# First slots of a fused attention, SoLU layer and gated layer kernel: softmax beside the first layer of the tile in front, values ahead of the next scores, products with x's low part last, w_out copies moved up

## The chip, the cores and the metric

The kernel runs on one core of one Trainium2 chip. The metric is the device time of one execution in microseconds (us). Engines are called as in the profile: PE is TensorE's matmul, PEld its weight load, DVE is VectorE, ACT is ScalarE, POOL is GpSimd, SP is SyncE, from whose queue most DMAs are issued.

## What is computed

Three layers follow one another on 4608 tokens: attention within chunks of 64 tokens (8 batches, 8 heads, head width 64), a layer with a softmax-weighted hidden vector and a layer norm, and a gated layer. Inputs q, k, v and g_ln are float32 as used here; the weights w_in, w_out, w_gate, w_val and w_out2 arrive as 8-byte numbers.

```python
scores = scale * np.matmul(q_c, k_c.transpose(0, 1, 2, 4, 3))
attn = np.exp(scores - max) ; attn = attn / (sum + 1e-09)
x = np.matmul(attn, v_c)            # 4608 x 512
h = x @ w_in                        # 4608 x 1024
sm = softmax(h); solu = h * sm
ln = (solu - mu) / np.sqrt(var + 1e-06) * g_ln
y = ln @ w_out                      # 4608 x 512
out = (silu(y @ w_gate) * (y @ w_val)) @ w_out2   # d_ff 1536
```

## The kernel before, in words

Tokens are taken as 36 tiles of 128; three tiles are a group. The first phase works through the tiles in slots, one for each t from 0 to 35; the second phase (from about 590 us on) is the gated layer over what the first phase left in DRAM.

Each float product is made of three: every operand is split into a high part and a low part (what the high part leaves over), and `PASSES` (L148) names the three products high by high, high by low, low by high.

The work on one tile t is a chain over four engines:

- `scores(t)` (L276): 32 small matmuls on PE into `s_ps`. `s_ps` and `o_ps` are two halves of one PSUM tile `so_ps` (L254, L255), and there is only one of it.
- `softmax(t)` (L281): DVE maximum (L283), DVE subtraction (L285), ACT exponential (L289). `softmax_b(t)` (L292): DVE sum, epsilon, reciprocal (L295, L296, L298), and the multiplication on POOL (L299).
- `p_transpose(t)` (L303): four PE transposes (L307) and an ACT copy p (L309). `pv(t)` (L312): 32 small matmuls with v into `o_ps`.
- `x_split(t)` (L317): ACT copies the high part of x (L321) and a DVE subtraction makes the low part, called later (L323).
- `hidden(t)` (L330): two halves of 12 products of 512 columns (L339) into the one PSUM tile `h`; in each half, for every k, high by high, high by low, low by high, in this order.
- `ln_max(t)` (L351, DVE), `ln_exp(t)` (L358, ACT), `ln_b(t)` (L364 to L373, DVE; its product at L369 is the last to read `h`), `ln_c(t)` (L379 on ACT, then seven instructions on POOL, L381 to L393).
- `ln_T(t)` (L409 on PE, L412 on ACT, and low parts on DVE, L417, called later).
- `y_run` (L155): products of the finished groups with w_out, `wB`, from slot 4 on (`Y_AT`).

Beside this the weights are converted from their 8-byte form: `conv_start` (L81, L87 on ACT, L94 on POOL) for the units of the next slot, `conv_b` (L100, L108 on DVE), `conv_c` (L129 on POOL), and for w_out `split_scaled` (L143 on ACT, L144 on DVE), which puts them into `wB`. Of w_out there are 8 units: one in each of the slots 0 to 3 and two in each of 4 and 5. A slot hands its units to the next as `todo2`; `steps[1]` is what calls `split_scaled` there. Units 0 to 3 hold the left half of w_out's columns (the first two y of a group), 4 to 7 the right half.

The order of instructions on each engine is written out by hand: from L506 on, every engine runs its instructions in the order in which the functions are called, and only data and buffers make it wait. In slots 0 to 3 (`first_slot`, L651) the order on PE is scores(t+2), pv(t+1), hidden(t), p_transpose(t+2), ln_T(t-1). In slots 4 to 35 (`slot`, L602) it is scores(t+2), hidden(t), ln_T(t-1), pv(t+1), y, p_transpose(t+2).

Loads go by SP's queue in the order of the calls: q and k of tile t+4, v of tile t+3, and at the end of a slot the raw weights for slot t+2.

Of the kernel before, what the change touches and what calls it, by code (L numbers as in the profile page):

```python
# [21 lines left out]
Y_AT = 4  # L22
# [4 lines left out]
def attn_moe_moe2_kernel(  # L27
# [13 lines left out]
    nc = tc.nc  # L41
# [4 lines left out]
    DM = 512  # L46
    KD = DM // P
# [100 lines left out]
    PASSES = ((0, 0), (0, 1), (1, 0))  # L148
# [37 lines left out]
    def w2_out(u):  # L186

        f, j = divmod(u, 3)
        if j == 0:
            gates[f] = stage.tile([P, 2, KH], F32, tag="ga", name="ga", bufs=2)  # L190
            return gates[f]
        if j == 1:
            blks[f] = stage.tile([P, 6, KH], F32, tag="blk", name="blk", bufs=1)
            return blks[f][:, 0:6:5]
# [43 lines left out]
    with ExitStack() as ph1:  # L238
        wpool = ph1.enter_context(tc.tile_pool(name="wpool", bufs=1))
        wA = wblock(wpool, "A", 2 * KD)  # L240
# [25 lines left out]
        def load_qk(t):  # L266
            qt[t] = att.tile([P, H, CH], F32, tag="qt", name="qt")
            nc.sync.dma_start(out=qt[t], in_=qT[t].rearrange("p (h i) -> p h i", h=H))
            kt[t] = att.tile([P, H, CH], F32, tag="kt", name="kt")
            nc.sync.dma_start(out=kt[t], in_=kT[t].rearrange("p (h j) -> p h j", h=H))  # L270

        def load_v(t):
            vt[t] = att.tile([P, H, CH], F32, tag="vt", name="vt")
            nc.sync.dma_start(out=vt[t], in_=v[t].rearrange("p (h d) -> p h d", h=H))

        def scores(t):  # L276
            q, k = qt.pop(t), kt.pop(t)
            for i in quads:
                quad(s_ps, q, k, *i)

        def softmax(t):  # L281
            mx = sm.tile([P, 2, NP], F32, tag="mx", name="mx")
            nc.vector.tensor_reduce(out=mx, in_=s_ps, axis=AX.X, op=ALU.max)  # L283
            e = att.tile([P, H, CH], F32, tag="e", name="e")
            nc.vector.tensor_tensor(  # L285
                out=e.rearrange("p (n c) j -> p c n j", c=2), in0=s_ps,
                in1=mx.unsqueeze(3).to_broadcast([P, 2, NP, CH]), op=ALU.subtract,
            )
            nc.scalar.activation(out=e, in_=e, func=AF.Exp, scale=SCALE)  # L289
            st[t] = e  # L290
# [21 lines left out]
        def pv(t):  # L312
            vv, p = vt.pop(t), st.pop(("p", t))
            for i in quads:
                quad(o_ps, vv, p, *i)

        def x_split(t):  # L317
            o = o_ps.rearrange("p c n i -> p n c i")
            x = xp.tile([P, 2, KD, P], F32R, tag="x", name="x")
            hi, lo = (x[:, i].rearrange("p n (c i) -> p n c i", c=2) for i in range(2))  # L320
            nc.scalar.activation(out=hi, in_=o, func=AF.Copy)  # L321
            xt[t] = x
            low = lambda: nc.vector.tensor_tensor(  # L323
                out=lo, in0=o, in1=hi.bitcast(F32), op=ALU.subtract
            )
            return low
# [3 lines left out]
        def hidden(t, halves=(0, 1)):  # L330
            x = xt[t]
            if 0 in halves:
                ht[t] = ps_h.tile([P, DF], F32, tag="h", name="h")
            h = ht[t]
            for n in halves:
                i = 0
                for k in range(KD):
                    for a, b in PASSES:
                        nc.tensor.matmul(  # L339
                            h[:, n * DM:(n + 1) * DM], lhsT=x[:, a, k, :],  # L340
                            rhs=wA[:, n * KD + k, b, :],
                            start=(i == 0), stop=(i == 3 * KD - 1),
                        )
                        i += 1
            if 1 in halves:
                del xt[t]

# [202 lines left out]
        x_low = x_split(0)  # L550
# [28 lines left out]
        x_low = x_split(1)  # L579
# [22 lines left out]
        def slot(t, todo2):  # L602


            todo, ahead = w_todo(t), t + 2 < NT
            cs = conv.pop(t)
            outs = [w2_out(u) if k == "2" else None for k, u in todo]
            if ahead:
                scores(t + 2)
                if t + 4 < NT:  # L610
                    load_qk(t + 4)
                softmax(t + 2)
            cs[:1] = [conv_c(c, o) for c, o in zip(conv_b(cs[:1]), outs)]
            if ahead:
                softmax_b(t + 2)
            if t > 0:
                hidden(t)
            ln_max(t)
            ln_exp(t)
            for k, steps in todo2:  # L620
                steps[0]()
            ln_low = ln_T(t - 1) if t >= 1 else None
            ln_b(t)
            x_low = None
            if t + 1 < NT:
                pv(t + 1)
                if t + 3 < NT:
                    load_v(t + 3)
                x_low = x_split(t + 1)
            if ln_low:  # L630
                ln_low()
            if x_low:
                x_low()
            ln_c(t)
            y0, y1 = y_upto(t - 1), y_upto(t)
            y2 = min(y1, -(-y0 // NY) * NY)
            y_run(wB, y0, y2, ps_y, att)
            for k, steps in todo2:
                steps[1]()
            if t + 1 < NT:  # L640
                conv_start(t + 1)
            cs[1:] = [conv_c(c, o) for c, o in zip(conv_b(cs[1:]), outs[1:])]
            y_run(wB, y2, y1, ps_y, att)
            for k, steps in todo2:
                steps[2]()
            if t + 2 < NT:
                raws[t + 2] = w_raw(t + 2)
                p_transpose(t + 2)
            return w_rest(todo, cs)

        def first_slot(t, todo2):  # L651


            todo = w_todo(t)
            cs = conv.pop(t)

            def attend():
                scores(t + 2)
                load_qk(t + 4)
                for k, steps in todo2:  # L660
                    steps[1]()
                softmax(t + 2)

            load_v(t + 3)
            if t > 0:
                attend()
                pv(t + 1)
                x_split(t + 1)()
                softmax_b(t + 2)
                conv_start(t + 1)  # L670
                hidden(t)
                p_transpose(t + 2)
            ln_max(t)
            ln_exp(t)
            cs = [conv_c(c) for c in conv_b(cs)]
            ln_low = ln_T(t - 1) if t > 0 else None
            ln_b(t)
            if t == 0:
                attend()
            if ln_low:  # L680
                ln_low()
            ln_c(t)
            if t == 0:
                softmax_b(t + 2)
                p_transpose(t + 2)
                conv_start(t + 1)
            raws[t + 2] = w_raw(t + 2)
            return w_rest(todo, cs)
# [254 lines left out]
```

## Time and profile before

| what | value |
|---|---|
| median of 3 runs | 1433.0 us (1431.76 to 1435.57) |
| the profiled execution, its own time | 1431.88 us |
| its span in the trace | 1430.1 us |
| PE busy | 1349.3 us, 94% of the span |
| DVE, ACT, POOL busy | 844.2, 565.5, 469.7 us |
| mean granted clock of TensorE | 0.982 |

The page cuts the span into 40 slices of 35.75 us. PE is busy for 90% or more of nearly every slice from the fifth on; the second and third slices, in which the first slots lie, are the ones with idle PE. A time "from the start" below is from the start of the span. In rows of the timeline, the bracket gives how long the engine was idle before the instruction and what ended that.

### The profile page before, as it was taken

To read this page: it belongs to the slowest core of one execution; us is meant where nothing else is said; L and a number is where in the kernel's file an instruction comes from. 1 tells how busy PE (TensorE), PEld (TensorE's weight loads), DVE (VectorE), ACT (ScalarE), POOL (GpSimd) and SP (SyncE) were. 2 spreads that over 40 slices of the span, in tenths; PEclk is the share of its full clock that TensorE was granted. 3 is DMA by queue.
4 is the path that set the end of the run, shared out by engine and by line. 5 is a ranking of instruction groups with operands and counts; after the bars stand their busy time and mean duration, and the time that the engine had idled before them with its cause. 6 is when DMAs were issued, how large, how long until landed. Compare 5 with 4: busy or idle time off the path is not lost.

```text
span 1430.1 us, 23605 instructions
## 1 busy us (share of the span) xinstructions
PE 1349.3 (94%) x9072; PEld 1231.2 (86%) x9072; DVE 844.2 (59%) x1540; ACT 565.5 (40%) x1144; POOL 469.7 (33%) x590
## 2 busy tenths in 40 slices
PE   3378999999999999899999999999999999999998
PEld 2367988888888889899989998999999999989997
DVE  6558577667777776455465456445544654474442
ACT  5346456446464545432242233223323323233231
POOL 5335354444545444421231223213212412141120
PEclk9689999999999999999999999999999999999999
DMA  6233265645555543886645473455455454735531
GB/s 235 67 118 108 77 207 164 205 153 196 175 194 177 190 146 119 302 319 231 232 145 190 173 241 138 173 195 210 148 198 205 156 189 166 246 127 181 202 106 45
DMA packets 91328, 252.15 MB, mean 176 GB/s; under 512 B 8272, under 2 KB 42064, under 8 KB 82000
## 3 DMA queue, kind: packets, MB, share of 16 engines
q1 hardware_dynamic: 84304, 241.21, 48.9%
q10 hardware_dynamic: 6912, 9.44, 1.9%
q8 instruction: 72, 1.18, 0.3%
q14 instruction: 40, 0.33, 0.1%
HBM read 203.43 MB, written 47.19 MB: 175 GB/s over the span
## 4 chain that ended last, share of the span: by engine, by line
PE 70%; DVE 2%; DMA 2%; ACT 1%; POOL 1%; issue 1%; ACTq 0%; SPq 0%; DVEq 0%; POOLq 0%
PE o L841 14%; PE pa L775 11%; PE pd L775 10%; PE pc L775 10%; PE tail L841 7%; PE h L339 6%; PE pb L775 5%; PE y L163 5%; PE so_ps L261 1%; PE tr L409 1%; DMA wsa<-ws 1%; DMA y<-ysb 1%; PE pt L307 1%; DVE so L369 0%; DVE nm L351 0%
## 5 line engine op out<-in xcount | busy, mean ns | idle before, releaser
L339 PE MATMUL h<-wA,x 128*128 128x512 f32 x864 | 217.0, 408 | 8.5 <-DVE x L323 2.8
L163 PE MATMUL y<-lnT,wB 128*128 128x384 f32 x1152 | 213.9, 343 | 9.4 <-ACT wB L143 5.7
L163 PEld LDWEIGHTS y<-lnT,wB 128*128 128x128 f32 x1152 | 202.6, 191 | 12.6 <-ACT wB L143 6.3
L832 POOL TENSOR_TENSOR uflow<-sa,uflow 128x384 fp32r<-128x384 f32 x72 | 73.4, 1019 | 414.0 <-ACT uflow L803 392.9
L339 PEld LDWEIGHTS h<-wA,x 128*128 128x128 f32 x864 | 165.7, 196 | 47.0 <-DVE x L323 3.6
L775 PE MATMUL pa<-yk,wsa 128*128 128x384 f32 x864 | 175.2, 337 | 3.4 <-ACT p L800 2.6
L775 PE MATMUL pd<-yk,wsb 128*128 128x384 f32 x864 | 173.0, 334 | 0.0
L832 DVE TENSOR_TENSOR uflow<-sb,uflow 128x128 fp32r<-128x128 f32 x72 | 28.1, 390 | 228.8 <-ACT uflow L830 228.8
L775 PEld LDWEIGHTS pa<-yk,wsa 128*128 128x128 f32 x864 | 153.2, 188 | 10.5 <-ACT p L800 2.9
L775 PEld LDWEIGHTS pd<-yk,wsb 128*128 128x128 f32 x864 | 151.8, 188 | 0.0
L811 POOL TENSOR_TENSOR u<-u,p 128x384 f32<-128x384 f32 x72 | 72.9, 1013 | 196.3 <-DVE u L810 183.7
L800 ACT ACTIVATE p<-pa 128x384 f32<-128x384 f32 x72 | 35.4, 492 | 234.1 <-PE pa L775 230.8
L841 PE MATMUL o<-wo,uflow 128*128 128x512 f32 x504 | 122.8, 392 | 0.0
L841 PEld LDWEIGHTS o<-wo,uflow 128*128 128x128 f32 x504 | 94.1, 188 | 18.0
L358 ACT ACTIVATE eh<-h,nm 128x1024 f32<-128x1024 f32 x36 | 40.2, 1117 | 143.7 <-DVE nm L351 143.7
L813 ACT ACTIVATE sa<-pa 128x384 f32<-128x384 f32 x72 | 35.4, 492 | 149.1 <-PE pa L775 149.1
L841 PE MATMUL o<-uflow 128*128 128x512 f32 x360 | 87.5, 392 | 0.0
L775 PE MATMUL pc<-yk,wsa 128*128 128x384 f32 x432 | 86.5, 334 | 0.0
L775 PE MATMUL pb<-yk,wsa 128*128 128x384 f32 x432 | 86.5, 334 | 0.0
L775 PE MATMUL pc<-yk,wsb 128*128 128x384 f32 x432 | 86.5, 334 | 0.0
L814 DVE TENSOR_TENSOR sa<-pa,sa 128x384 f32<-128x384 f32 x72 | 40.2, 558 | 71.5 <-ACT sa L813 71.5
L841 PEld LDWEIGHTS o<-uflow 128*128 128x128 f32 x360 | 67.3, 188 | 13.1
(106 smaller groups left out, 2282.6 us busy)
## 6 DMA issues: line engine op xcount, KB each, us to landing
wsa<-ws SPq DMA_DIRECT2D x72, 1024.0 KB, 5.1
wsb<-ws SPq DMA_DIRECT2D x72, 768.0 KB, 6.0
ws<-shi SPq DMA_DIRECT2D x12, 896.0 KB, 4.4
raw<-in_moe_w_out SPq DMA_DIRECT2D x20, 512.0 KB, 6.6
qt<-in_q SPq DMA_DIRECT2D x36, 256.0 KB, 4.1
kt<-in_k SPq DMA_DIRECT2D x36, 256.0 KB, 4.0
vt<-in_v SPq DMA_DIRECT2D x36, 256.0 KB, 2.8
y<-ysb ACTq DMA_DIRECT2D x48, 192.0 KB, 2.4
```

The costliest lines, as they stand in the source:

```text
L163: nc.tensor.matmul(ys[u], lhsT=wB[:, f, a, d * P:(d + 1) * P], rhs=lnT[m][:, b, f, :], start=(n == 0), stop=(n == NY - 1),)
L261: nc.tensor.matmul(out[b * CH:(b + 1) * CH, c, n], lhsT=lhsT[r, h], rhs=rhs[r, h], start=True, stop=True, tile_position=(c * CH, b * CH),)
L307: nc.tensor.transpose(pt[:, 2 * n:2 * n + 2].rearrange("p h i -> p (h i)"), e[:, n], ident)
L339: nc.tensor.matmul(h[:, n * DM:(n + 1) * DM], lhsT=x[:, a, k, :], rhs=wA[:, n * KD + k, b, :], start=(i == 0), stop=(i == 3 * KD - 1),)
L358: nc.scalar.activation(out=e, in_=h, func=AF.Exp, bias=nm, accum_out=se)
L775: nc.tensor.matmul(ps, lhsT=w[:, a, kk * P:(kk + 1) * P], rhs=yk[:, i, b, kk], start=(first and n == 0), stop=(n == 5), skip_group_check=True,
L800: nc.scalar.activation(out=p1, in_=psA, func=AF.Copy)
L811: nc.gpsimd.tensor_tensor(out=u3, in0=u3, in1=p5, op=ALU.add)
L813: nc.scalar.activation(out=sa, in_=psA, func=AF.Sigmoid)
L814: nc.vector.tensor_tensor(out=sa, in0=psA, in1=sa, op=ALU.mult)
L832: sub = lambda eng, o, x, h: eng.tensor_tensor(out=o, in0=x, in1=h.bitcast(F32), op=ALU.subtract)
L841: nc.tensor.matmul(o, lhsT=u[:, a, i * P:(i + 1) * P], rhs=wout(f)[:, b], start=(j0 and j == 0), stop=(j1 and j == 2),)
```

## The change

It does five things, and nothing else of the kernel is touched.

1. In `hidden`, the products of a half are put in another order: first, for every k, high by high and high by low of x's high part, and after these eight the four with x's low part. The number of products is the same.
2. In the first slots, softmax(t+1), w_out's split, softmax_b(t+1) and conv_start(t+1) come at the head of slot t, beside hidden(t), and p_transpose(t+1) behind hidden(t). Before, slot t held the softmax of tile t+2, whose scores stood in the same slot; now its scores come one slot ahead of it.
3. In the first slots, pv(t+1) now stands after ln_T(t-1) and ahead of scores(t+2); q, k and v are loaded after these, x's high part is copied then, its low part is made after ln_b(t) and ahead of ln_T's low parts.
4. Slot 4 (`t == Y_AT`) takes up the shifted order: it begins with softmax(5), softmax_b(5), hidden(4), p_transpose(5), and goes on with scores(6) and softmax(6) as before.
5. In `slot`, w_out's splits (of slots 4, 5 and 6) move from behind ln_c to behind softmax_b(t+2), ahead of hidden(t) and ln_max(t).

```diff
             for n in halves:
-                i = 0
-                for k in range(KD):
-                    for a, b in PASSES:
-                        nc.tensor.matmul(
...
+                order = [(k, 0, b) for k in range(KD) for b in range(2)]
+                order += [(k, 1, 0) for k in range(KD)]
+                for i, (k, a, b) in enumerate(order):
+                    nc.tensor.matmul(
...
             outs = [w2_out(u) if k == "2" else None for k, u in todo]
+            if t == Y_AT:
+                softmax(t + 1)
+                softmax_b(t + 1)
+                hidden(t)
+                p_transpose(t + 1)
             if ahead:
                 scores(t + 2)
...
             if ahead:
                 softmax_b(t + 2)
-            if t > 0:
+            for k, steps in todo2:
+                if k == "o":
+                    steps[1]()
+            todo2 = [x for x in todo2 if x[0] != "o"]
+            if t > Y_AT:
                 hidden(t)
...
             todo = w_todo(t)
             cs = conv.pop(t)
-
-            def attend():
-                scores(t + 2)
-                load_qk(t + 4)
+            if t > 0:
+                softmax(t + 1)
                 for k, steps in todo2:
                     steps[1]()
-                softmax(t + 2)
-
-            load_v(t + 3)
-            if t > 0:
-                attend()
-                pv(t + 1)
-                x_split(t + 1)()
-                softmax_b(t + 2)
+                softmax_b(t + 1)
                 conv_start(t + 1)
                 hidden(t)
-                p_transpose(t + 2)
+                p_transpose(t + 1)
             ln_max(t)
             ln_exp(t)
             cs = [conv_c(c) for c in conv_b(cs)]
             ln_low = ln_T(t - 1) if t > 0 else None
+            x_low = None
+            if t > 0:
+                pv(t + 1)
+            scores(t + 2)
+            load_qk(t + 4)
+            load_v(t + 3)
+            if t > 0:
+                x_low = x_split(t + 1)
             ln_b(t)
-            if t == 0:
-                attend()
-            if ln_low:
+            if t > 0:
+                x_low()
                 ln_low()
             ln_c(t)
             if t == 0:
-                softmax_b(t + 2)
-                p_transpose(t + 2)
                 conv_start(t + 1)
             raws[t + 2] = w_raw(t + 2)
             return w_rest(todo, cs)
```

## Rows read from the trace of the kernel before

**Rows 1.** Two stretches: busy time of each engine, granted clock, DMA share, GB/s.

```profile
60.00:80.00 20.00, 13.39 (x118) 11.08 (x117) 9.47 (x19) 7.18 (x13) 5.82 (x10) 0.83 0.34 108
180.00:200.00 20.00, 20.00 (x185) 17.40 (x174) 15.46 (x26) 11.37 (x21) 11.43 (x16) 1.00 0.86 278
```

**Rows 2.** Timeline of PE: start, length, line, tiles, count, idle before.

```profile
48.61 1.12 PE L307 MATMUL pt<-ident,e 128*128 128x128 f32 x4 [11.27 <-POOL e L299]
55.26 7.32 PE L339 MATMUL h<-wA,x 128*128 128x512 f32 x24
71.12 1.13 PE L261 MATMUL so_ps<-p,vt 64*64 64x64 f32 x32 [6.61 <-issue]
72.18 7.35 PE L339 MATMUL h<-wA,x 128*128 128x512 f32 x24
79.37 0.60 PE L307 MATMUL pt<-ident,e 128*128 128x128 f32 x4
80.77 0.70 PE L261 MATMUL so_ps<-kt,qt 64*64 64x64 f32 x32
101.02 5.72 PE L339 MATMUL h<-wA,x 128*128 128x512 f32 x24 [2.49 <-DVE so L369]
142.05 8.98 PE L163 MATMUL y<-lnT,wB 128*128 128x384 f32 x36 [4.28 <-ACT wB L143]
152.01 5.75 PE L339 MATMUL h<-wA,x 128*128 128x512 f32 x24
```

**Rows 3.** Timeline of ACT, DVE and POOL in slots 2 and 3.

```profile
68.28 0.89 ACT L143 ACTIVATE wB<-m,g_sb 128x256 fp32r<-128x256 f32 x2
68.81 0.89 DVE L144 SCALAR_TENSOR_TENSOR wB<-m,g_sb,wB 128x256 fp32r<-128x256 f32 x2 [0.57 <-ACT wB L143]
70.33 0.69 DVE L285 TENSOR_TENSOR e<-so_ps,mx 128x512 f32<-128x512 f32 x1
71.05 0.63 ACT L289 ACTIVATE e<-e 128x512 f32<-128x512 f32 x1 [1.88 <-DVE e L285]
73.55 0.68 DVE L295 TENSOR_REDUCE su<-e 128x8 f32<-128x512 f32 x1
74.83 1.04 POOL L299 TENSOR_TENSOR e<-e,r 128x512 f32<-128x512 f32 x1 [2.97 <-DVE r L298]
80.01 0.60 ACT L309 ACTIVATE p<-pt 128x512 f32<-128x512 f32 x1 [5.96 <-PE pt L307]
80.89 1.11 ACT L358 ACTIVATE eh<-h,nm 128x1024 f32<-128x1024 f32 x1 [0.29 <-DVE nm L351]
81.16 0.69 DVE L108 SCALAR_TENSOR_TENSOR m<-raw,m 128x512 int32<-128x512 int32 x1
82.52 1.28 DVE L369 SCALAR_TENSOR_TENSOR so<-h,rh,eh 128x1024 f32<-128x1024 f32 x1
83.91 1.28 DVE L417 TENSOR_TENSOR lnT<-tr,lnT 128x512 fp32r<-128x512 f32 x2
```

**Rows 4.** Timeline around the end of the prologue: PE, then DVE.

```profile
35.99 0.73 PE L339 MATMUL h<-wA,x 128*128 128x512 f32 x2 [0.22 <-DVE wA L501]
39.64 1.28 DVE L369 SCALAR_TENSOR_TENSOR so<-h,rh,eh 128x1024 f32<-128x1024 f32 x1
```

**Rows 5.** Timeline, a DVE and a POOL instruction that overlap in slot 5.

```profile
118.16 1.68 DVE L108 SCALAR_TENSOR_TENSOR m<-raw,m 128x512 int32<-128x512 int32 x1
117.81 1.48 POOL L129 TENSOR_TENSOR m<-m,raw 128x512 int32<-128x512 int32 x1
```

**Rows 6.** DMA issues from 62 to 90 us: count, size, median us to landing.

```profile
raw<-in_moe_w_out SPq DMA_DIRECT2D x2, 512.0 KB, 6.6
```

**Rows 7.** Timeline of DVE in slots 4 and 5; the page's row on y.

```profile
109.73 1.28 DVE L369 SCALAR_TENSOR_TENSOR so<-h,rh,eh 128x1024 f32<-128x1024 f32 x1
121.45 1.17 DVE L351 TENSOR_REDUCE nm<-h 128x1 f32<-128x1024 f32 x1
L163 PE MATMUL y<-lnT,wB 128*128 128x384 f32 x1152 | 213.9, 343 | 9.4 <-ACT wB L143 5.7
```

More of the change, by code (lines that the diff above doesn't have):

```diff
@@ L335, in hidden @@
             for n in halves:
-                i = 0
-                for k in range(KD):
-                    for a, b in PASSES:
-                        nc.tensor.matmul(
[L340 to L344, printed above, removed]
+                order = [(k, 0, b) for k in range(KD) for b in range(2)]
+                order += [(k, 1, 0) for k in range(KD)]
+                for i, (k, a, b) in enumerate(order):
+                    nc.tensor.matmul(
+                        h[:, n * DM:(n + 1) * DM], lhsT=x[:, a, k, :],
+                        rhs=wA[:, n * KD + k, b, :],
+                        start=(i == 0), stop=(i == 3 * KD - 1),
+                    )
             if 1 in halves:
```

## The prediction

> **What bounds the kernel now.** I read first the page's slices and two stretches of 20 us cut from them: at 180 to 200 us PE is busy for all 20.00 us, at 60 to 80 us for 13.39, at a granted clock of 0.83 [rows 1]. So nearly everywhere PE sets the time, and only the first slots have room. Then the timeline of PE there. hidden(1) to hidden(4) start at 55.26, 72.18, (89.13) and 101.02 us: a first slot takes 17 us, though its products take 7.3, and hidden(1) itself comes 18 us after the prologue, after an idle stretch of 11.27 us that ends with a softmax multiplication on POOL [rows 2]. Then what PE waits for. pv at 71.12 stands idle for 6.61 us "issue" and starts 0.07 us after softmax's exponential, that is right behind the subtraction (70.33 + 0.69 = 71.02) [rows 2, 3]: scores and values share one PSUM tile, so pv(t+1) waits until DVE has read scores(t+2), and these were queued behind all of ln_b, ln_T's low parts and the split. hidden(t) stands behind pv, and so softmax and hidden run one after the other. hidden then takes 7.35 us, not 5.72, because the clock has fallen to half (1.2 of 2.4 GHz) in the idle stretch [rows 2]. Slot 6 shows another wait: y stands for 4.28 us until the last split of w_out, and its 36 products take 8.98 us, 0.249 each, against 213.9/1152 = 0.186 over the kernel [rows 2, 7]. From 152 us on PE is the bound.
>
> **The change, slot by slot.** I call M(t) the end of L369 for tile t: from there h is free for hidden(t+1). Before, M(0) = 39.64 + 1.28 = 40.92 [rows 4].
>
> *Order of the products, prologue.* The last block of w_in is ready at 35.99; two products follow it [rows 4]. In the new order five do: 3 more at 0.24 is 0.72 us later, which was hidden in the wait for the weights. Everything from ln_max(0) moves by that: M(0) = 41.64. In all other tiles x's low part is there in time, before and after; the 24 products stay 24, so 5.72 stays 5.72, and I cost it at nothing (range: 0 to -0.4 us in a first slot, where hidden need not wait for the low part, off the path).
>
> *Slot 0 and 1.* Nothing of attention stands ahead of hidden(1) any more; its x is there since the prologue. It starts 0.16 us after M(0) (101.02 against the end of the tile before, as the row's wait on L369 shows), at 41.8 instead of 55.26. PE is idle from about 38.1 (scores(2), which stay behind hidden(0)) to 41.8, 3.7 us. An idle stretch of 2.49 us left the clock up, one of 4.28 us did not [rows 2]; 3.7 is nearer to the latter, so I take 7.32 us for hidden(1): end 49.1. Then ln_max to the start of the exponential 80.89 - (72.18 + 7.35) = 1.36, and from there to M 82.52 - 80.89 + 1.28 = 2.91 [rows 2, 3]. M(1) = 53.4. softmax(2) beside it is done sooner (its p at about 49.8).
>
> *Slots 2 and 3.* Two branches lead from M(t-1) to the exponential of tile t. By hidden: 0.16 + 5.72 to 7.35 + 1.36 = 7.2 to 8.9 us. By softmax of t+1, since ACT's queue holds the copy p(t+1) ahead of ln_exp(t) and DVE's the low parts ahead of softmax: 0.11 to x's low part, 0.64 (half of a pair of 1.28), 1.28 for ln_T's low parts, 0.72 for the maximum (as the subtraction), 0.72 to the exponential, 0.63; 0.53 until the split's low parts can start, 0.89; 1.28 from the sum to the multiplication on POOL, 1.04; transposes 0.06 + 0.60, p 0.60 [rows 2, 3]. Together 9.1 us, later than the first branch even at the lower clock. With 2.91 to M the period is 12.0 us. It is no less than 10.1 (the branch by hidden, warm).
>
> What may come on top. The split's low parts now meet the POOL work of ln_c. A DVE sign pass that takes 0.69 alone took 1.68 when it began 0.35 us behind a POOL addition [rows 3, 5]; here the overlap by my walk is 0.3 to 0.9 us, and I take 0.5: period 12.5. Bounds 0 and 1.0.
>
> The Trainium skill has this as a rule (SBUF — State Buffer, "Who interferes with whom"): a DVE instruction with two inputs in SBUF and a GpSimd instruction that reads SBUF share a read port, and whichever comes second stands until the first is through. Rows 5 agree (1.68 for 0.69). By the rule alone the slot would be 12.3 to 12.9, without it 12.0.
>
> *DMAs.* q, k and v of later tiles now leave behind scores and pv; they are used two slots later, some 20 us, which covers them. The raw w_out of slot t+1 is another matter: it leaves near M(t-1), behind q, k and v on SP, and ACT's copy p(t+1) stands behind its conversion. With two units (issued in slot 2 for slot 4, converted in slot 3) it lands 6.6 us later [rows 6]; two units of conversion (four ACT passes of about 0.6) then end near 9.2 instead of p's place at 8.5, so 0.6 for slot 3 alone; bounds 0 and 2. With one unit the landing fits, at nothing.
>
> So M(2) = 53.4 + 12.5 = 65.9 and M(3) = 65.9 + 12.5 + 0.6 = 79.0. hidden(4) starts at 79.2 instead of 101.02.
>
> *Slot 4* pays something back: two softmaxes now stand in it. From M(3): to the end of softmax(5)'s exponential 4.1; sum to multiplication's end 2.3; transposes 0.7; scores(6) 0.7; maximum and subtraction 1.44; shift and sign, at most 0.69 each, about 1.1 together; sum chain 1.1; split's low parts 0.9; then 1.36 and 2.91 to M(4). That is 16.5 us: M(4) = 95.5. hidden(4) is long done by then, so ln_max(4) waits for DVE, and scores(7), hence hidden(5), wait for x's low part of tile 5 behind M(4).
>
> *Slot 5.* Before, from M(4) (109.73 + 1.28) to ln_max(5) it took 10.44 us, DVE without a pause worth naming [rows 7]. Of that one unit's split goes (0.9) and two units' come in (1.7), two waits of about a us in sum go: 10.1 + 1.36 + 2.91 = 14.4. M(5) = 109.9. PE has 13 us of work in it and waits for DVE.
>
> *Slot 6.* From M(5): x's low part 2.0, scores(8) 0.7, hidden(6) 5.7, transposes of ln 1.0, pv 0.7, 48 products of y at 0.186 = 8.9 with no wait any more (the last split is done near 9.7, y starts at 10.1), transposes and scores 1.3: 20.3. hidden(7) starts at 130.2 instead of 152.01: **21.8 us** sooner. The moved splits cost nothing further: DVE has the rest of slot 6, in which PE sets the pace again.
>
> *After that* PE is the bound, as at 180 to 200 us [rows 1], every load is issued by the progress of the slots, and nothing is tied to absolute time; the rest is shifted as it is.
>
> Sum: the profiled execution took 1431.88 (span 1430.1, and 1.8 around it), so 1410.1 for such a one. The median of the runs is 1.1 above it: 1411.
>
> **The rivals.**
>
> *Closer to PE's bound.* If DVE and ACT keep up, slots 1 to 3 fall to 10.1 to 12.0, and slots 4 to 6 to PE's own work (14.3, 13.0, 17.4): 5 to 9 us more, 1402 to 1406. For it: PE's part of a slot is only 8.7. Against: ACT's order has p ahead of ln_exp, and the walk on that side is made of measured lengths.
>
> *Longer slots.* Hidden(1) to (3) cold, each contention at its upper bound and the raw units late by 2 us: 1.0 x 3 + 1.4 + slots 4 and 5 with 2 us more each, since all that DVE does there is on the path: 6 to 9 us less, 1416 to 1421.
>
> *No change.* The change doesn't do what it says: pv(t+1) ahead of scores(t+2) still waits, for instance because copying x's high part now has to wait for scores(t+2) (one PSUM tile). I price that wait: 0.7 us, and ACT is busy with ln_T's copies then. To eat all, each of six slots would have to lose 3.6 us more. 1429 to 1437.
>
> *Slower.* The products' order holds for all 36 tiles, and from tile 7 on PE is the bound. If x's low part last made a product slower (it alternates less between the two parts of x, and the weights are loaded anew for each product in either order), the price would be 29 tiles x 24 products x the loss. It decides from 21.8/696 = 0.031 us a product, 0.239 becoming 0.270. I know of no row that speaks for it. At 0.040 us a product 1439.
>
> **How the numbers follow.** The forecast, slots of 12 to 13 us and the waits in slots 4 and 5, 1406 to 1416: 0.62. Closer to PE's bound: 0.12. Longer slots: 0.19. No change: 0.03. Slower: 0.04. The range leaves out the two last and the ends of the others: 1403 to 1420. A measurement of this kernel tells some 0.3% (4 us) from no change; by that bound faster 0.93, same 0.03, slower 0.04.
>
> **What the profile after would show.** hidden(1) near 41.8 us, hidden(2) and (3) 12 to 13 us apart, p(t+1) on ACT directly ahead of ln_exp(t) and, in slots 2 and 3, the last thing it waits for; hidden(4) near 79, hidden(5) near 98, hidden(7) near 130; no wait of y for the split in slot 6; hidden's 24 products at 5.7 us from slot 7 on, and a span from hidden(7) to the end as before (1278 us). The prediction is wrong if hidden(1) doesn't come at once after tile 0's ln_b, if slots 4 and 5 take back over 10 us by DVE's queue, or if the rest from hidden(7) on has another length.

## The result and the profile after

Over four runs the changed kernel takes 1411.21 us (1409.87 to 1413.74) against 1432.38 us for the kernel before on the same chip: ratio 0.9852, 95% interval 0.9829 to 0.9875, so 21.2 us faster. Forecast were 1411. The profiled execution took 1411.09 us with a span of 1409.3, 20.8 less than before. (In the changed kernel the lines from L351 to L417 have moved up by one: the product that frees `h` is L368, the maximum L350, ln_T's low part L416. `M(t)` is, as in the prediction, the end of L368 for tile t.)

The total is as forecast; its parts are not. Up to hidden(7) the gain is 16.6 us where 21.8 were forecast, and behind hidden(7) 4.2 more came where none was.

| us | before | forecast | after |
|---|---|---|---|
| M(0) | 40.92 | 41.64 | 42.79 |
| hidden(1) starts, takes | 55.26, 7.32 | 41.8, 7.32 | 42.95, 7.83 |
| M(1), M(2), M(3) | 66.84, 83.80, 100.86 | 53.4, 65.9, 79.0 | 55.04, 66.96, 80.62 |
| hidden(4) | 101.02 | 79.2 | 80.78 |
| M(4) | 111.01 | 95.5 | 98.22 |
| hidden(5) | 115.48 | about 98 | 101.33 |
| M(5) | 125.57 | 109.9 | 114.81 |
| hidden(7) | 152.01 | 130.2 | 135.45 |
| hidden(7) to the end of the span | 1278.1 | 1278 | 1273.9 |

First the stretches, as in [rows 1]: stretch, its length, busy time of PE, PEld, DVE, ACT, POOL, granted clock, DMA share, GB/s. The prologue's end of before, then four of after.

```profile
20.00:40.00 20.00, 10.90 (x92) 6.85 (x92) 17.27 (x26) 10.24 (x18) 11.37 (x10) 0.95 0.32 102
```

```profile
20.00:40.00 20.00, 12.70 (x92) 8.30 (x92) 15.81 (x22) 9.24 (x18) 10.56 (x9) 0.67 0.22 67
60.00:80.00 20.00, 11.94 (x180) 9.47 (x179) 14.51 (x29) 12.04 (x23) 9.24 (x14) 1.00 0.29 94
100.00:120.00 20.00, 18.16 (x167) 15.53 (x168) 16.10 (x27) 11.97 (x24) 11.00 (x19) 0.86 0.28 89
150.00:170.00 20.00, 20.00 (x162) 17.43 (x162) 16.24 (x30) 8.94 (x15) 9.60 (x13) 1.00 0.40 129
```

At 60 to 80 us PE now does 180 instructions in 11.94 us at full clock, where before it did 118 in 13.39 at 0.83: more work, in less busy time. From 150 us on it is busy throughout, as before at 180. The prologue has got worse: the same 92 instructions keep PE busy for 12.70 us instead of 10.90, at a granted clock of 0.67 instead of 0.95.

The timeline of PE after (start, length, idle time before and what ended it):

```profile
35.36 3.23 PE L339 MATMUL h<-wA,x 128*128 128x512 f32 x6 [0.36 <-ACT wA L496]
42.95 7.83 PE L339 MATMUL h<-wA,x 128*128 128x512 f32 x24 [3.30 <-DVE so L368]
55.20 5.70 PE L339 MATMUL h<-wA,x 128*128 128x512 f32 x24 [2.02 <-DVE so L368]
67.12 5.72 PE L339 MATMUL h<-wA,x 128*128 128x512 f32 x24 [1.62 <-DVE so L368]
80.78 5.73 PE L339 MATMUL h<-wA,x 128*128 128x512 f32 x24 [1.73 <-DVE so L368]
100.27 1.13 PE L261 MATMUL so_ps<-kt,qt 64*64 64x64 f32 x32 [4.83 <-DVE x L323]
101.33 7.65 PE L339 MATMUL h<-wA,x 128*128 128x512 f32 x24
116.85 0.70 PE L261 MATMUL so_ps<-kt,qt 64*64 64x64 f32 x32 [1.57 <-DVE x L323]
124.66 8.60 PE L163 MATMUL y<-lnT,wB 128*128 128x384 f32 x48
135.45 5.75 PE L339 MATMUL h<-wA,x 128*128 128x512 f32 x24
```

Against [rows 2]: the idle 11.27 and 6.61 us are gone, the y that stood 4.28 us for the split now runs its 48 products without a break, and hidden(2) and hidden(3) are warm, that is, run at the full clock (5.7 us). In their place stand waits of about 2 us for `so` (the end of ln_b of the tile before), and in slot 5 a new one of 4.83 us: scores(7) waits for x's low part, which lies in DVE's queue, and hidden(5) behind it is cold, that is, run at the lower clock (7.65 us; 5.74 before). The waits of PE from 30 to 140 us in sum (us in total, times, longest):

```profile
PE h L339 <- DVE so L368: 8.7, 4, 3.3
PE so_ps L261 <- DVE x L323: 6.4, 2, 4.8
PE pt L307 <- POOL e L299: 4.4, 3, 2.0
```

All three end on DVE or on what DVE feeds.

### The profile page after: what moved, and what is told of

Its sections match the earlier page's. It is cut to its first block, busy times and chain, and to the rows that moved or that the text cites. A ratio compares the mean times of both kernels' runs of the same rounds, so it can differ in the third digit from the quotient of the medians.

```text
span 1409.3 us, 23612 instructions
## 1 busy us (share of the span) xinstructions
PE 1344.0 (95%) x9072; PEld 1226.5 (87%) x9072; DVE 847.8 (60%) x1540; ACT 565.3 (40%) x1144; POOL 468.4 (33%) x590
## 4 chain that ended last, share of the span: by engine, by line
PE 70%; DVE 2%; ACT 1%; POOL 1%; issue 1%; DMA 0%; ACTq 0%; SPq 0%; DVEq 0%; POOLq 0%
PE o L845 14%; PE pa L779 11%; PE pc L779 11%; PE pd L779 11%; PE tail L845 7%; PE pb L779 5%; PE y L163 5%; PE h L339 5%; PE so_ps L261 1%; PE tr L408 1%; DVE so L368 1%; DVE nm L350 1%; PE pt L307 0%; DVE blk L218 0%; ACT eh L357 0%
## 5 line engine op out<-in xcount | busy, mean ns | idle before, releaser
L163 PE MATMUL y<-lnT,wB 128*128 128x384 f32 x1152 | 210.7, 340 | 3.7 <-DVE lnT L416 3.7
```

Of the source, the lines that this page charges most:

```text
L163: nc.tensor.matmul(ys[u], lhsT=wB[:, f, a, d * P:(d + 1) * P], rhs=lnT[m][:, b, f, :], start=(n == 0), stop=(n == NY - 1),)
```

## The experiments

**The theory** after this result: the shifted slots bring the gain; the order of the products costs some 2 us in the prologue; slots 4 and 5 lose the rest by DVE's queue; and the 2.8 us at the start of the second phase come from the order of the products as well. **Rivals**: the products' order itself brings part of the gain in the slots; the moved splits of w_out bring it, or cost nothing; the difference behind hidden(7) is chance.

### The parts of the change, each alone and each taken out

**a1_order_only**: the kernel before with the new order of the products, nothing else.

```diff
-                i = 0
-                for k in range(KD):
-                    for a, b in PASSES:
+                order = [(k, 0, b) for k in range(KD) for b in range(2)]
+                order += [(k, 1, 0) for k in range(KD)]
+                for i, (k, a, b) in enumerate(order):
```

> The kernel before, with only the new order of hidden's products. Theory (a fixed price in the prologue): the first half ends sooner, the second later, since five products instead of two stand behind the last block of w_in; M(0), the end of L369 for tile 0 (40.92 us before, 42.79 in the changed kernel), comes 0.7 us later if the clock stays up and 1.9 if the idle time ahead of the second half lets it fall to half, as in the changed kernel; all else is shifted by that and hidden's 24 products stay at 5.7 us from slot 7 on: span 1431 to 1432. Rival (the order acts on every tile): the shift between hidden(7) and the end of the span changes by several us, either way.

Measured: 1431.98 us, ratio 0.9992 (0.9983 to 1.0001). M(0) at 43.01 instead of 40.92, hidden(7) at 154.43 instead of 152.01, hidden(35) at 560.68 instead of 558.25. So 2.1 us are lost in the prologue, 2.4 by hidden(3), and they stay lost through the whole first phase. Yet the span is 1429.8, 0.3 less than before: the second step of the second phase, whose first product `pa` was at 605.75, now starts at 605.44. There 2.7 us come back.

**a2_old_order**: the changed kernel with the old order (the same edit the other way).

> The changed kernel with hidden's products back in their old order. Theory: M(0) back at 40.9 instead of 42.8 us, hidden(0) ends at 36.7 instead of 38.6, and hidden(1) to hidden(7) start 1.9 us sooner, less at most 0.4 us in a slot where hidden's third product now waits for x's low part; hidden(7) near 133.6, span 1407 to 1408. Rival (the order is what the first slots need, since the low part is made behind ln_b): hidden(2) to (4) lose 1 us or more each, and hidden(7) starts at 136 us or later.

Measured: 1414.43 us, ratio 0.9865 (0.9848 to 0.9881), span 1412.4. M(0) at 40.67; hidden(1), (2), (3), (4) at 40.83, 52.61, 64.67 and 77.61, hidden(7) at 133.73, 1.7 us sooner than in the changed kernel. From hidden(1) to hidden(4) it takes 36.8 us, with the new order 37.8: so the order brings nothing in slots 1 to 3, and for them this rival falls. From hidden(4) to hidden(7) this kernel takes 56.1 us and the changed one 54.7; whether that is the order isn't shown, since hidden(4), (5) and (6) are all cold here (7.47, 7.17 and 7.35 us). That this kernel is nonetheless 3.2 us slower lies behind hidden(7): 1.9 us are lost by tile 35 (hidden(35) at 540.54 against 540.34; the clock, as shown further below), and 2.8 more at the second step of the second phase (its `pa` at 588.05 against 585.03).

**a3_split_only**: the kernel before with w_out's splits moved up in slots 4 to 6.

```diff
             if ahead:
                 softmax_b(t + 2)
+            for k, steps in todo2:
+                if k == "o":
+                    steps[1]()
+            todo2 = [x for x in todo2 if x[0] != "o"]
             if t > 0:
                 hidden(t)
```

> The kernel before, with only w_out's splits moved ahead of hidden and ln_max in slots 4 to 6. Theory: y's wait of 4.28 us in slot 6 and its 36 products at the lower clock (2.3 us) go, while ln_max in slots 4 and 5 comes up to 0.9 and 1.7 us later behind the splits in DVE's queue: hidden(7) starts at 147 to 149 us instead of 152.0, span 1425 to 1427. Rival (DVE is as full as PE there): PE waits for ln_b instead, hidden(7) at 151 to 153, span 1429 to 1431.

Measured: 1428.67 us, ratio 0.9979 (0.9962 to 0.9995). hidden(7) starts at 150.26, 1.75 us sooner. hidden(6) starts 4.0 us later than before (132.28 against 128.24): what y no longer waits for in slot 6, PE mostly waits for in slot 5, where DVE now has the split ahead of ln_max and of x's low part. In the profiled execution even the 1.75 us are lost again by tile 35 (558.20 against 558.25); the median is 3.9 us lower. The nine executions lie in two groups, five from 1426.26 to 1428.67 us with a mean granted clock of 0.983 to 0.986, four from 1431.98 to 1434.16 with 0.977 to 0.982; the profiled one is of the second, and no trace shows where the first gains.

**a4_split_back**: the changed kernel with the splits back behind ln_c (the four added lines of a3 out).

> The changed kernel with w_out's splits back behind ln_c in slots 4 to 6. Theory: M(4) and M(5) come 0.9 and 1.7 us sooner (fewer passes ahead of ln_max), and in slot 6 y waits for the last split again, about 4 us, and runs cold: hidden(7) at 136 to 139 us instead of 135.45, span 1410 to 1413. Rival (the moved splits cost more on DVE's queue than they save): hidden(7) at 134 or sooner, span 1408 or less.

Measured: 1418.9 us (1413.69 to 1420.08), ratio 0.9894 (0.9873 to 0.9915). M(4) comes 2.2 us sooner (96.04; 0.6 of it was there by M(3), ahead of the edit), hidden(5) at 101.92, hidden(6) at 114.53 (12.6 us behind it, instead of 16.2), but hidden(7) only at 137.62: y waits for the split twice, 8.9 us together in slots 4 and 6. So the moved splits are worth 2.8 us from hidden(4) to hidden(7): 5.1 less in slot 6, 3.5 more in slot 5, 1.2 less in slot 4. The rival is half right: they help, and they are not free. The larger part, hidden(7) from 152.01 to 137.62 with the prologue's loss still in it, is the shifted slots; the three parts of that shift (2 to 4 of the change) were not run apart. The median lies 7.7 us above the changed kernel's, the profiled execution (span 1411.9) only 2.6; it was the fastest of this kernel, with a mean granted clock of 0.988 where the other three had 0.981 to 0.984.

### What the late parts wait for

**b1_raw_first**: the changed kernel, but in slots 1 and 2 the raw w_out loads go into SP's queue ahead of q, k and v.

```diff
+            if t in (1, 2):
+                raws[t + 2] = w_raw(t + 2)
             scores(t + 2)
...
-            raws[t + 2] = w_raw(t + 2)
+            if t not in (1, 2):
+                raws[t + 2] = w_raw(t + 2)
```

> The changed kernel, but in slots 1 and 2 the raw w_out loads stand ahead of q, k and v on SP's queue, so that they leave as soon as SP is free and land some 10 us sooner. Theory (slot 3 is long because ACT's copy p(4) stands behind the conversion of two units that land late): ACT's two waits for the raw loads in slot 3 (2.48 and 0.65 us) go, and M(3) comes 11.9 us after M(2), as M(2) after M(1), not 13.66: hidden(4) 1.7 us sooner, near 79.0, and hidden(5) to (7) with it; span 1407.6. Rival (slot 3 is bound by its softmax branch and the DMAs' congestion moves elsewhere): hidden(4) stays at 80.3 or later.

Slot 3 of the changed kernel took 13.66 us, slot 2 took 11.92. ACT's timeline in slot 3 of the changed kernel says why:

```profile
74.23 0.68 ACT L81 ACTIVATE m<-raw 128x512 f32<-128x512 f32 x1 [2.48 <-DMA raw<-in_moe_w_out]
75.56 0.69 ACT L81 ACTIVATE m<-raw 128x512 f32<-128x512 f32 x1 [0.65 <-DMA raw<-in_moe_w_out]
77.26 0.57 ACT L309 ACTIVATE p<-pt 128x512 f32<-128x512 f32 x1
77.74 1.09 ACT L357 ACTIVATE eh<-h,nm 128x1024 f32<-128x1024 f32 x1
```

ACT stands 2.48 and 0.65 us for the raw loads, and the copy p and the exponential queue right behind. In b1 the same copy comes at

```profile
75.19 0.60 ACT L309 ACTIVATE p<-pt 128x512 f32<-128x512 f32 x1 [1.26 <-PE pt L307]
```

Measured: 1409.66 us, ratio 0.9833 (0.981 to 0.9857). Slot 3 takes 11.99 us, hidden(4) starts at 78.84, 1.94 sooner, and hidden(7) at 133.53, 1.92 sooner. So the raw loads cost 1.7 us in slot 3, and the gain arrives whole at hidden(7); the median is 1.6 us lower. The price is not a fixed one. In the kernels that issue these loads late, ACT's first wait for them and the length of slot 3 go together: 0.57 and 11.87 us in b5, 1.40 and 12.62 in b2, 1.74 and 12.94 in a2, 2.10 and 13.28 in a4, 2.48 and 13.66 in the changed kernel, 3.79 and 14.93 in b3. So part of what these kernels seem to gain or lose by slot 3 is this wait and not their own edit.

**b2_ln_first**: the changed kernel, but in slot 4 ln_max(4) and ln_exp(4) are called ahead of scores(6), softmax(6) and the split.

```diff
                 hidden(t)
                 p_transpose(t + 1)
+                ln_max(t)
+                ln_exp(t)
...
-            ln_max(t)
-            ln_exp(t)
+            if t != Y_AT:
+                ln_max(t)
+                ln_exp(t)
```

> The changed kernel, but in slot 4 ln_max(4) and ln_exp(4) stand ahead of scores(6) and softmax(6). Theory (slot 4 is long, 17.6 us from M(3) to M(4), because ln_max(4) waits in DVE's queue behind two softmaxes, though hidden(4) is done 7.5 us before): the maximum, the exponential and their latency (2.6 us) leave the chain to M(4): M(4) near 95.5 instead of 98.2, hidden(5) to (7) 2.7 us sooner, hidden(7) near 132.8, span 1406.6. Rival (DVE has that much work in slots 4 and 5 in any order): the gain at hidden(5) is gone at hidden(7), 134.5 or later.

DVE's timeline, the maximum of tile 4 and the product that ends at M(4), first of the changed kernel, then of b2:

```profile
94.01 1.21 DVE L350 TENSOR_REDUCE nm<-h 128x1 f32<-128x1024 f32 x1
96.94 1.28 DVE L368 SCALAR_TENSOR_TENSOR so<-h,rh,eh 128x1024 f32<-128x1024 f32 x1
```

```profile
85.28 1.23 DVE L350 TENSOR_REDUCE nm<-h 128x1 f32<-128x1024 f32 x1 [0.78 <-PE h L339]
93.13 1.28 DVE L368 SCALAR_TENSOR_TENSOR so<-h,rh,eh 128x1024 f32<-128x1024 f32 x1
```

Measured: 1406.41 us, ratio 0.9813 (0.9795 to 0.9831). Slot 4 takes 15.05 us instead of 17.60; M(4) is 3.8 us sooner (94.41; 1.3 of it was there by M(3), by the shorter wait for the raw loads). hidden(7) starts at 133.10, 2.35 us sooner, and only 1.1 of that is the edit's: slot 5, again of 16.6 us, ends in a wait of 3.93 us for x's low part, behind which hidden(6) is cold (7.98 us). DVE's queue is what sets these slots.

### The prologue and the start of the second phase

**b3_tile0_old**: the changed kernel, old order in tile 0 alone.

```diff
                 order += [(k, 1, 0) for k in range(KD)]
+                if t == 0:
+                    order = [(k, a, b) for k in range(KD) for a, b in PASSES]
```

> The changed kernel with the old order of products in tile 0 alone. Two things are asked. Prologue: M(0) at 40.7 to 40.9 instead of 42.8, hidden(7) 1.7 to 2.1 us sooner, near 133.6. Start of the second phase, theory (the builder's assignment of the eight DMA completion counters in turn follows tile 0's order, and the first load of wsb then shares one with the store of the last group's first y): SP's wait of about 8 us for that store ahead of the first wsb, and PE's wait of 2.6 us in the second step, are back as in every kernel with the old order; the first two products into pa are 6.9 us apart, not 4.2; span 1410 to 1411. Rival (it is the order in the last tiles that does it, or chance): they are 4.2 us apart, span 1407.5.

Measured: 1415.58 us, ratio 0.9881 (0.9856 to 0.9905). M(0) is 1.46 us sooner (41.33), but slot 3 is longer (14.93, by the raw loads), hidden(7) at 137.18; the profiled execution (1419.51) is the slowest of the four. And the first two `pa` of the second phase lie 6.57 us apart again (585.33 and 591.90). So what separates the two products at the start of the second phase is tied to tile 0's order, some 560 us earlier. It is not chance.

What waits there is seen in the queues. ACT's and SP's issues and PE at that place, before:

```profile
594.70 0.32 SPq L743 DMA_DIRECT2D wsb<-ws  x1
595.59 0.40 SPq L742 DMA_DIRECT2D wsa<-ws  x1
604.84 0.33 ACTq L170 DMA_DIRECT2D y<-ysb  x1
605.21 0.49 ACT L800 ACTIVATE p<-pa 128x384 f32<-128x384 f32 x1 [3.30 <-DMA wsa<-ws]
605.75 1.33 PE L775 MATMUL pa<-yk,wsa 128*128 128x384 f32 x6 [2.62 <-ACT p L800]
```

and after:

```profile
570.10 0.32 SPq L746 DMA_DIRECT2D wsa<-ws  x1
582.74 0.33 ACTq L170 DMA_DIRECT2D y<-ysb  x1
583.12 0.49 ACT L804 ACTIVATE p<-pa 128x384 f32<-128x384 f32 x1 [1.55 <-PE pc L779]
585.03 1.20 PE L779 MATMUL pa<-yk,wsa 128*128 128x384 f32 x6
```

and what SP waited for, before, after and in b3 (us, times, longest):

```profile
SPq L743 <- DMA y<-ysb: 7.9, 1, 7.9
```

```profile
SPq L743 <- DMA y<-ysb: 5.6, 1, 5.6
```

```profile
SPq L749 <- DMA y<-ysb: 8.2, 1, 8.2
```

Before, SP stands for 7.9 us until the first y of the last group has landed, right ahead of issuing the weights `wsb`; ACT stands 3.30 us until a weight load has landed, and this is just ahead of the last store of y, with ACT's copy of `pa` and then PE behind it. Neither wait is one of data. In the programs as built, the loads and stores of SP and ACT take eight completion counters in turn, and a DMA is not issued before the one that used its counter last has landed. Before, the first store of the last group uses the same counter as the first load of `wsb` (L743 before); with the new order it comes four places later in the program's list of DMAs, and SP's wait falls on a load of `wo` (L743 after), which is needed later. The last store of y shares its counter with the second load of `wsa` in both. Before, that load is issued behind SP's wait, at 595.59, and ACT stands for it; after, it has left ahead of SP's wait, at 570.10, and PE loses nothing. All programs bear this out. Those in which the store shares its counter with `wsb` (before, a2, a3, b3, and b6 below) have 6.6 to 7.0 us between the two `pa`; those in which it shares with `wo` (after, a1, a4, b1, b2, and b4 and b5 below) have 4.1 to 4.2. Why the order of a few products moves the store in the list is not shown.

The Trainium skill (DMA: Bandwidth & Descriptors, "Anatomy of one DMA — SWDGE (gpsimd) path", so written of DMAs that GpSimd issues) says that DMA engines don't wait on semaphores and that any such wait stands on the issuing sequencer; the trace agrees for ACT's queue, since here it holds up an engine's arithmetic: ACT's copy starts 0.04 us behind the store's issue, 605.21 against 604.84 + 0.33.

**b5_half1_old**: the changed kernel, old order in the second half of tile 0 alone (the condition is `t == 0 and n == 1`).

> The changed kernel with the old order in the second half of tile 0 alone; there the counters come out as in the changed kernel. Theory: the second half ends with two products behind w_in's last block, but at the lower clock, since the first half is still done early: hidden(0) ends near 37.0 instead of 38.6, M(0) near 41.2, hidden(7) 1.4 us sooner, near 134.0; the first two products into pa stay 4.2 us apart; span 1407.5 to 1408. Rival (the price in the prologue is the clock's, by the idle time behind the first half, and not the number of products behind the last block): M(0) stays at 42 or later and nothing is gained.

Measured: 1411.2 us, ratio 0.985 (0.9826 to 0.9874). PE at the prologue's end:

```profile
31.91 4.75 PE L341 MATMUL h<-wA,x 128*128 128x512 f32 x12
36.59 0.69 PE L261 MATMUL so_ps<-kt,qt 64*64 64x64 f32 x32
```

The second half, started at 31.91, ends at 36.66 instead of 38.59, though the clock was down as in the changed kernel for part of it (granted 0.55 from 32 to 36 us; before 1.00). M(0) comes at 40.86, as before the change. So the loss comes of how many products stand behind the last block of weights, and the low clock makes each of them dear. hidden(7) starts at 132.10, 3.35 us sooner than in the changed kernel (1.93 by M(0); slot 3, with its short wait for the raw loads, brings 1.8, and 0.4 are lost again), and the two `pa` are 4.2 us apart. Yet the span is only 1.7 us shorter (1407.6), since 1.7 us are lost between hidden(7) and the end, most of it to the clock (below). The median is the same; the profiled execution is the fastest of the four.

### Versions that put it together

**b4_all**: b1, b2 and b5 in one kernel.

> The changed kernel with the three edits together that shortened it one by one: raw loads first in slots 1 and 2, ln_max(4) and ln_exp(4) ahead of scores(6), and the old order of products in the second half of tile 0. Theory (the three lie on one chain and add up): hidden(4) near 76.9 (80.78 less 1.9 and 2.0), hidden(5) near 93.2, hidden(7) near 129.2 instead of 135.45, and the same 4.2 us between the first two products into pa; span 1403. Rival (they take their gain from the same wait): hidden(7) at 131 or later.

Measured: 1405.89 us, ratio 0.9819 (0.9805 to 0.9832). hidden(4) at 78.05, hidden(7) at 131.81. The three don't add up: from hidden(4) to hidden(7) it still takes 53.8 us, 54.7 in the changed kernel. From M(3) to M(4) 2.1 us are gained; from M(4) to M(5) it takes 16.6 us as there, bound by DVE's queue; then scores(8) waits 3.90 us for x's low part, hidden(6) is cold (8.11 us), and 1.6 are lost again.

**b6_split5_late**: b4 with the splits of slot 5 alone back behind ln_c.

```diff
+            if t != Y_AT + 1:
                 for k, steps in todo2:
                     if k == "o":
                         steps[1]()
```

> As the last kernel, and in slot 5 alone the splits of units 4 and 5 go back behind ln_c; units 3, 6 and 7 stay early. Theory (slot 5 is bound by DVE's queue from M(4) to ln_max(5), in which these four passes take 2.4 us, and nothing needs them before slot 6): hidden(6) and hidden(7) come 2.4 us sooner still, hidden(7) near 126.8. The counters of the DMAs fall as in the old order here: by the theory of the shared counter, SP's wait ahead of the first wsb and PE's 2.2 to 2.7 us in the second step return, so the span is 1403 all the same. Rival for the first: y in slot 6 now waits for units 4 and 5, and hidden(7) stays at 129; rival for the second: 4.2 us between the first two products into pa, span 1400.5.

Measured: 1406.77 us, ratio 0.982 (0.9807 to 0.9833). Slot 5 (M(4) to M(5)) falls from 16.60 to 14.23 us, hidden(7) starts at 127.50, 4.3 us sooner, and no y waits for it. But the two `pa` are 6.86 us apart again (571.28 and 578.14), with SP's wait of 7.9 us: the counters have shifted once more, this time with the order as in b4. So it is not the products' order as such that decides there.

**b7_store_sp**: b6, with the last group's y stored from SP's queue instead of ACT's.

```diff
-                nc.scalar.dma_start(out=y_dram[m][d], in_=ysb)
+                (nc.sync if m == NG - 1 else nc.scalar).dma_start(out=y_dram[m][d], in_=ysb)
```

> As the last kernel, but the four y of the last group are stored from SP's queue, not ACT's. Theory (the loss at the start of the second phase is that ACT stands in its own queue at the store of a y, which waits for the counter of a late weight load, so that the copy p behind it is late): ACT has no such wait any more, the first two products into pa are 4.2 us apart, span 2.5 us less than in the last kernel, near 1400.5. Rival (PE waits for the weights themselves): 6.5 to 6.9 us apart as before, span 1403; or the stores delay the loads on SP, and PE waits for these.

Measured: **1402.94 us** (1402.02 to 1404.72), ratio 0.9797 (0.9784 to 0.981), below both kernels and 8.3 us under the changed one. The copy of `pa` and the second `pa`:

```profile
573.52 0.49 ACT L813 ACTIVATE p<-pa 128x384 f32<-128x384 f32 x1 [0.50 <-PE pa L788]
576.45 1.20 PE L788 MATMUL pa<-yk,wsa 128*128 128x384 f32 x6
```

ACT now copies right behind the product, PE goes on without a break, and the two `pa` are 4.17 us apart.

## Why the prediction was right, and where it was not

The forecast case came (1406 to 1416), by its main mechanism: with softmax(t+1) beside hidden(t), the periods of the first slots fall from 17 to 12 us. The total, 1411, is within 0.3 us; but two errors of opposite sign are in it, 5.25 us too little gain up to hidden(7) and 4.24 too much behind it.

*Start of hidden(1).* Right: 0.16 us behind M(0), PE idle ahead of it (3.30 us), and cold (7.83 us; forecast 7.32, [rows 2]).

*Order of the products, prologue.* Right in sign, too small: 1.87 us where 0.72 was forecast. "3 more at 0.24" took the number of products behind the last block for a full clock. Six products from that block on took 3.23 us, 0.54 each, against two in 0.73 [rows 4], at a granted clock of 0.50 from 28 to 40 us; before it was 1.00 from 24 to 36. What the clock's fall follows here: the first half's twelve products end at 26.38 instead of 28.93, and PE then stands 2.83 us.

*Order of the products in the slots.* Costed at nothing, and a2 bears it out for slots 1 to 3: 36.8 us with the old order, 37.8 with the new. For slots 4 to 6 it stays open (a2).

*Slots 2 and 3.* Slot 2 took 11.92 us; forecast 12.5, of which 0.5 was for contention. The split's two low parts began 0.45 us ahead of the end of POOL's last instruction of ln_c, and took 1.11 us where 0.89 stood in [rows 3]: 0.22 of contention, and the other terms came 0.3 shorter in sum than their 12.0. The rule of the Trainium skill (SBUF — State Buffer, "Who interferes with whom") agrees in direction; the 12.3 to 12.9 that it alone would have made of the slot did not come. The end of the chain is as walked: in slot 2, p and the exponential are neighbours on ACT, as forecast.

```profile
63.57 0.60 ACT L309 ACTIVATE p<-pt 128x512 f32<-128x512 f32 x1 [2.48 <-PE pt L307]
64.06 1.11 ACT L357 ACTIVATE eh<-h,nm 128x1024 f32<-128x1024 f32 x1
```

For slot 3 the raw loads were named as the cause and put at 0.6 us; by b1 they cost 1.7, inside the upper bound of 2 (in b3 2.9, above it). The 6.6 us of [rows 6] was taken for a landing that would stay; the loads now take 7.4 us.

*Slots 4 and 5.* Right in the main that DVE's queue sets them, and that x's low part holds up PE; both too short, 17.60 us against 16.5 and 16.59 against 14.4. (The terms listed for slot 4 add up to 16.6.) In slot 5 all that is missing lies between M(4) and ln_max(5): 12.44 us, forecast 10.1 out of 10.44 before. Two terms of that sum failed.

The first is a wait. One split less (0.9) and two waits less (about 1 us) were to bring 1.9 to 2.0 us, but DVE's second pair of conversion passes starts 5.95 us behind M(4), where before it was 6.29 (117.30 - 111.01): 0.34 gained. It needs POOL's L94, and POOL comes to that only behind all of ln_c(4). With the split out of its way DVE just waits longer there. The prediction walked DVE's queue and left out POOL's. DVE before, then DVE and POOL after:

```profile
117.30 0.83 DVE L100 TENSOR_SCALAR m<-m 128x512 int32<-128x512 int32 x1 [0.27 <-POOL m L94]
```

```profile
104.17 0.83 DVE L100 TENSOR_SCALAR m<-m 128x512 int32<-128x512 int32 x1 [1.21 <-POOL m L94]
108.33 2.41 DVE L144 SCALAR_TENSOR_TENSOR wB<-m,g_sb,wB 128x256 fp32r<-128x256 f32 x4
110.66 1.21 DVE L350 TENSOR_REDUCE nm<-h 128x1 f32<-128x1024 f32 x1
```

```profile
103.53 1.19 POOL L94 TENSOR_SCALAR m<-m 128x512 f32<-128x512 f32 x2
108.58 1.08 POOL L299 TENSOR_TENSOR e<-e,r 128x512 f32<-128x512 f32 x1 [0.43 <-DVE r L298]
```

The second is contention: the four low parts of the two units take 2.41 us instead of 1.7. Right behind softmax_b they meet POOL's multiplication L299, which is released by the same reciprocal on DVE; four of them took 1.68 us in slot 6 before, and take 1.69 in b6, where they stand behind ln_c. Slot 4 has the same: its two low parts took 1.62 us where 0.9 was forecast, 0.7 of the 1.1 us missing there. The same rule of the Trainium skill fits this; the prediction had priced it in slots 2 and 3 and not here. b6, which takes the splits out of slot 5, makes it 2.4 us shorter (14.23 against 16.60).

*Slot 6.* 20.6 us from M(5) to hidden(7), forecast 20.3; y waits for no split, as the steps said, and its 48 products take 8.60 us. The page's row on y says it for the whole kernel: the 9.4 us idle ahead of it in [rows 7], most of it for the split, have become 3.7 us for ln_T's low part.

```profile
L163 PE MATMUL y<-lnT,wB 128*128 128x384 f32 x1152 | 210.7, 340 | 3.7 <-DVE lnT L416 3.7
```

*"Nothing is tied to absolute time; the rest is shifted as it is."* This step failed, by the prediction's own sign of being wrong: the rest has another length, 4.24 us less. 2.8 of it is the second step of the second phase, shown by a1 and b3 to hang on tile 0's order and by the queues to be a wait for a completion counter. That no data tie the parts together was true; that nothing does was not. The other 1.4 us lie between hidden(7) and hidden(35), and go with TensorE's clock. Five times in these slots PE waits for 1.9 to 2.4 us (once 3.05, in a3), at the same places in every kernel, and behind some of these waits hidden runs cold. Before, this happens twice (hidden(14) takes 7.34 us, hidden(17) 6.28), in the changed kernel once (hidden(14), 6.52). Over all kernels the stretch takes 403.2 to 403.4 us where it never happens (b2, b4, b6, b7), 404.9 and 405.3 where it happens once (the changed kernel, a4), and 406.2 to 407.9 where twice (the other seven). The same wait ahead of hidden(14), before and in b7 (granted clock 0.65 from 252 to 256 us and 1.00 from 229 to 235):

```profile
251.54 0.63 PE L307 MATMUL pt<-ident,e 128*128 128x128 f32 x4 [1.88 <-POOL rs L392]
252.72 7.34 PE L339 MATMUL h<-wA,x 128*128 128x512 f32 x24
```

```profile
227.84 0.63 PE L307 MATMUL pt<-ident,e 128*128 128x128 f32 x4 [1.89 <-POOL rs L393]
229.03 5.78 PE L341 MATMUL h<-wA,x 128*128 128x512 f32 x24
```

What decides whether the clock falls there stays open; the four kernels in which it doesn't all have b2's edit.

So the 1411 was met with some luck: neither the shift of the counters nor the one cold hidden less was forecast. Without the first it would have been some 2.8 us more, without both 4.2, 1414 to 1415 by this sum, still inside the range.

*The rivals.* "Closer to PE's bound" did not come, since ACT in slot 3 and DVE and POOL in slots 4 and 5 do not keep up; b7, in which these slots are shorter and ACT's store is out of the way, takes 1403. "Longer slots" is right for slots 3 to 5 and cost 3.85 us there (0.56, 1.1 and 2.19), too little for its 1416 to 1421. "Slower" by the order of the products is out: 5.7 us for 24 products from slot 2 on.

## What to carry to other kernels

When work is moved off a critical chain, walk every queue to which it is moved: here the split was taken out of PE's way in slot 6 and put into DVE's way in slot 5, and the best version treats the two slots differently (b6). When a wait is removed, the neighbours in the same in-order queue decide what comes next, and a wait for another engine behind them can take up all that was gained (slot 5); a load that feeds ACT, issued behind loads that are used two slots later, held up everything behind it. And a store issued from an engine that also computes can stop this engine for as long as some earlier DMA is under way: look for arithmetic that starts right behind a DMA issue.

## What the runs showed of the hardware that was not expected

Reordering products of tile 0 moved a wait of SP's queue from one load to another, some 560 us later (7.9 us ahead of `wsb`, then 5.6 ahead of `wo`), worth 2.7 to 2.8 us (a1, a2). The wait is real in the traces; that it is one of completion counters is read from the programs, and b7 shows that what PE loses there hangs on the store in ACT's queue (4.17 us between the two `pa` instead of 6.86).

The clock of TensorE fell behind an idle time of 2.83 us in the prologue, where the work around it was sparse (granted 0.50 from 28 to 40 us), and stayed at 1.00 in the slots with waits of 1.62 and 2.02 us (60 to 80 us). The length of one idle time doesn't decide it: in the prologue of the kernel before PE stood for 2.84 us ahead of 25.05, and the clock stayed at 1.00 (20 to 36 us); ahead of hidden(14) a wait of 1.88 us was followed by 0.65 before, one of 1.89 by 1.00 in b7. Twelve products that show no wait take 4.75 us when part of them run at the low clock (b5), while six products at 0.50 took 3.23.
